# Gated linear attention and a convolution-gated feed-forward: new rules for the planner that orders the instructions, and new priorities

## The chip, the core and the metric

The kernel runs on one core of a Trainium2 chip. A core has five engines with an instruction queue each: TensorE (PE in the profile; its weight loads are PEld), VectorE (DVE), ScalarE (ACT), GpSimd (POOL) and SyncE (SP, which here issues every transfer). Each engine takes its queue strictly in order and waits on semaphores for the others. The metric is the device time of one execution in microseconds (us), the median of several; lower is better.

## The reference, cut to what matters

Inputs: `q`, `k`, `v`, `f_logit` of 4 batches x 8 heads x 768 steps x 48, in float32, and three weights that arrive as 64-bit floats and are split into float32 parts in the kernel.

```python
f = 1.0 / (1.0 + np.exp(-f_logit))
for t in range(768):                       # gated linear attention, state is 48 x 48 per head
    state = f[:, :, t, :, None] * state + np.einsum('bhd,bhe->bhde', k[:, :, t], v[:, :, t])
    y[:, :, t] = np.einsum('bhd,bhde->bhe', q[:, :, t], state)
x = y, heads side by side                  # 4 x 768 x 384
h = np.maximum(x @ w_in, 0.0)              # 384 -> 1024
conv_out = sum over k of conv_w[k] * hp[:, k:k + S, :]   # 3 taps along the sequence, hp is h padded
gate = 1.0 / (1.0 + np.exp(-conv_out))
out = (h * gate) @ w_out                   # 1024 -> 384
```

## The kernel before, in words

**Attention.** The 768 steps of a batch are cut into 6 chunks of 128, which makes 24 chunks in all. For a chunk, SP loads the logits `fb`, the pair k and q as one tile `kq`, and `v`. ACT takes Exp and Ln of the logits (L374, L376; from the tenth chunk on for three chunks at once), DVE forms the running sum along the chunk (the scan, L392), ACT takes the two exponentials `e` (L395, L397), and DVE multiplies them into `kq` (the product, L401). TensorE then multiplies k with q head by head into the one PSUM tile `A` (the score, L418, eight products in sixteen matmul records), and DVE copies the lower triangle of it into `am` (the mask copy, L421). TensorE adds up the output `Y` from the carried state (the carry, L433) and from `am` and `v` (the value step, L440). It also transposes k (L407), which is copied to `kp` by whichever of ACT and DVE is free first (L410), and multiplies it with `v` (the rank step, L462) for the next state, which DVE completes (L469 to L474). ACT and DVE split `Y` into a high and a low part in `xT` (L450, L452). Some rows of `xT` are moved by six small transfers per half batch (L482).

**Feed-forward.** The unit is half a batch, three chunks. Each unit has eight first-layer steps of nine matmuls (L512), one per block of 128 hidden features; each is followed by Relu (ACT, L522), three taps (one on ACT, L528, two on DVE, L532), and for every two blocks a Tanh (ACT, L536) and the gate product (DVE, L538). Each tile of 128 output rows then takes a high part (ACT, L555), a low part (DVE, L559), 24 second-layer matmuls (L568: sixteen with the high part, eight with the low part), a copy (ACT, L574) and a store. There are 64 first-layer steps and 24 tiles.

**Weights.** `w_in` comes in six pieces and `w_out` in eight, as 64-bit floats. `split_f64` turns each piece into a high and a low float32 by a chain of small operations (L287 to L311) that mostly feed each other on DVE; for eleven of the fourteen pieces TensorE joins the low part with three matmuls (L316 to L318, the join).

**What sets the order.** Nothing is issued while the code above runs. Each step becomes an `Op` with an engine (or two to choose from), a duration, a priority key, the steps it needs and the buffers it takes. `Plan.order` then plays the whole program through with a small model: an engine that is free takes the ready step of the lowest key whose buffers are free. `PIPE` is how much before its end a step on ACT or DVE lets the next one start, `LAT` is how long after its end other engines see it. The keys are a step's chunk or unit number plus an offset from the table `CFG` (`f` for the logit loads, `gate` for Exp and Ln, `a` for scan, exponentials and product, `sc` for score and mask copy, `m1` and `m2` for the layers, `w1`, `w1s`, `w2`, `w2s` for weights). The steps are issued in the order in which the plan starts them. In the plan before, a step that needs the result of the step just ahead of it on the same engine may start as early as one that does not (`free[e]`, the time with `PIPE` taken off, is passed as the `"soon"` event).

```python
o.start, o.on, o.end = now, e, now + ns
free[e] = o.end - self.PIPE[e]
seen = o.end + self.LAT[e]
```

Of the kernel before, what the change touches and what calls it, by code (L numbers as in the profile page):

```python
# [11 lines left out]
F32 = mybir.dt.float32  # L12
# [4 lines left out]
AF = mybir.ActivationFunctionType  # L17
ALU = mybir.AluOpType
# [5 lines left out]
F_MIN = 2.0 ** -64  # L24
CFG = dict(lf=3, sg=3, nf=6, groups=[3, 3, 3, 3, 3, 3, 3, 3], f=(-10.52, -14.9), gate=(-0.4, 2.24), kq=-8.44, v=2.32,
           a=5.05, ft=-1.2, b=0.88, sc=-1.11, va=-0.4, st=0.74, ga=-12.99, w1=(-1.96, 2.97),
           w1s=(4.07, 0.42, -5.53, 1.16, 3.36, 1.3), cw=-19.7, w2=(10.23, 8.77),
           w2s=(2.31, 3.44, 5.42, 5.13, 6.56, 6.96, 7.77, 5.53),
           m1=(-1.06, 0.62, 1.0, 0.51, -0.31, 0.54, -0.47, -1.02), m1d=1.83,
           m2=(-0.72, -1.09, 1.03, 0.42, 1.64, -1.82, 0.47, 2.64), m2d=1.96, ez='dddddddddddvvv')  # L30

# [7 lines left out]
class Plan:  # L39

    LOOSE = ("mm", "s", "low", "ob")
    LAT = dict(PE=210, ACT=50, DVE=50, POOL=100, SP=60)
    PIPE = dict(PE=0, ACT=100, DVE=80, POOL=0, SP=0)

# [30 lines left out]
    def order(self):  # L75
        now = 0.0
        free = {e: 0.0 for e in self.LAT}
# [5 lines left out]
        seq = 0  # L83
        done, dma, pipe, mode, table = [], [], 0.0, None, "NE"
        for o in self.ops:
# [4 lines left out]
        while events:  # L90
            now = events[0][0]
            while events and events[0][0] <= now:
                _, _, o = heapq.heappop(events)
# [15 lines left out]
            for e in free:  # L109
# [4 lines left out]
                for o in sorted(ready[e], key=lambda o: o.key):  # L114
# [3 lines left out]
                    for r, i in o.take:  # L118
# [3 lines left out]
                        b = next((b for b in self.rings[r] if not (b[1] & taken)), None)  # L122
# [18 lines left out]
                ns = o.engs[e]  # L141
                if e == "PE":
                    if mode == "r" and o.mode == "f":
                        ns += 95
                    mode = o.mode
                if e == "ACT" and o.mode and o.mode not in table:
                    table = {"N": "N", "T": "TE", "E": "TE"}[o.mode]
# [3 lines left out]
                seen = o.end + self.LAT[e]  # L151
                if e == "SP":
                    pipe = max(o.end + 1500, pipe) + o.size / 0.34
                    seen = pipe + 700
                    dma.append(seen)
                    heapq.heappush(events, (seen, seq, None))
                done.append(o)
                for k, (t, w) in enumerate(((free[e], ("soon", o)), (seen, ("done", o)), (seen, ("free", o)))):
                    seq += 1
                    heapq.heappush(events, (t, seq, w))  # L160
# [11 lines left out]
def gla_moe_kernel(ctx, tc, kq_in, v_in, f_in, w_in, conv_w, w_out, out):  # L172


    nc = tc.nc
# [8 lines left out]
    groups = CFG["groups"]  # L184
# [43 lines left out]
    plan, serial = Plan(), count()  # L228
# [12 lines left out]
    cw = const.tile([P, 3, NF], F32, name="cw")  # L241
# [30 lines left out]
    def split_f64(raw, at, r, n, key, need, hi, lo, nm, mode=None):  # L272
        ids = ("raw", raw), ("ms", nm), ("low", nm), ("mm", "pz" + nm)
        x = n / 512
# [7 lines left out]
        def step(eng, ns, run, need, use=(0, 1), take=()):  # L282
            return plan.op(eng, ns, lambda e: run(e), key, need=need, use=[ids[i] for i in use],
                           take=[(("raw", "ms", "low", "mm")[i], ids[i]) for i in take])

        V, A = nc.vector, nc.scalar
        o = step("ACT", 160 + 500 * x, lambda e: A.activation(ms(0).bitcast(F32), pr(1).bitcast(F32), AF.Abs), [need],  # L287
                 use=(0,), take=(1,))
# [8 lines left out]
                 use=(1,))  # L297
# [6 lines left out]
        if mode == "v":  # L304
            o = step("DVE", 150 + 530 * x, lambda e: V.scalar_tensor_tensor(
                sf(), pr(0).bitcast(U32), 2.0 ** -52, sf(), ALU.mult, ALU.mult), [s])
            o = step("DVE", 150 + 530 * x, lambda e: V.tensor_tensor(mf(), mf(), hi().bitcast(F32), ALU.subtract), [h, o],
                     use=(1,))
            return step("DVE", 150 + 530 * x, lambda e: V.tensor_tensor(lo(), mf(), sf(), ALU.add), [o], use=(1,))
        low = lambda: plan.buf(ids[2])[:, :n]  # L310
# [49 lines left out]
    for g, m in enumerate(groups):  # L360
        fb = ("fb", g)
# [18 lines left out]
    for n in range(N):  # L380
# [13 lines left out]
        ev = lambda z, E=E: buf(E)[:, z].rearrange("p n t -> p (n t)")  # L394
        o1 = plan.op("ACT", 600, lambda e, fv=fv, ev=ev: nc.scalar.activation(ev(0), fv(), AF.Exp), ka, need=[o], use=[fb],  # L395
                     take=[("e", E)], mode="E")
        o2 = plan.op("ACT", 600, lambda e, fv=fv, ev=ev: nc.scalar.activation(ev(1), fv(), AF.Exp, scale=-1.0), ka,  # L397
                     need=[o, o1], use=[fb, E], mode="E")
        keep = plan.op("POOL", 400, lambda e, E=E, b=b, c=c: nc.gpsimd.tensor_copy(ft_all[:, b, c, :], buf(E)[:, 1, :, P - 1]),
# [8 lines left out]

        o = plan.op("PE", 450, turn, kb, need=[ox], use=[X], take=[("s", pt)], mode="f")
        okp = plan.op(dict(ACT=580, DVE=685), 0, lambda e, KP=KP, pt=pt: (  # L410
# [25 lines left out]
        def value(e, c=c, Y=Y, V=V, AM=AM):  # L436
            for p, j in heads:
# [5 lines left out]
        oc = plan.op("PE", 590, carry, kv, need=[stated[n - 1], ox], use=[X], take=[("Y", Y)], mode="f") if c else None  # L443
        ov = plan.op("PE", 1024, value, kv, need=[o, oc, ld_v], use=[V, AM] + ([Y] if c else []),
                     take=[] if c else [("Y", Y)], mode="f")
# [8 lines left out]
        if c < NC - 1:  # L454
# [9 lines left out]

            o = plan.op("PE", 595, rank, ks, need=[ov, okp], use=[KP, V, Y], mode="f")
            ft = ft_all[r, b, c, :].rearrange("p (n o) -> p n o", o=1).broadcast_to([HP + D, NP, D])
# [278 lines left out]
```

## Time and profile before

| what | value |
|---|---|
| time, median of 3 runs | 347.39 us (346.68 to 348.35) |
| the profiled execution's own time | 346.48 us |
| its span, first to last instruction | 344.8 us |
| TensorE busy (records) | 316.0 us, 92% |
| VectorE busy | 282.5 us, 82% |
| ScalarE busy | 237.5 us, 69% |
| GpSimd busy | 24.6 us, 7% |
| mean granted TensorE clock | 0.988 |

The share of busy time is an average over stages. The page's 40 slices show VectorE at nine tenths or more in most slices up to 210 us and at four to eight tenths later, and TensorE the other way round: gaps in the first 50 us, few after 100 us. The transfers move 390 to 410 GB/s in the second to fourth slice (8.6 to 34.5 us) and mostly under 140 GB/s from the sixth on.

### The profile page before, as it was taken

The page shows a single profiled execution, that of the slowest core. Times are in us where ns is not written, and L with a number is a line of the kernel's source. Part 1 is how long each engine was busy: PE and PEld are TensorE (multiplying, and loading weights), DVE is VectorE, ACT ScalarE, POOL GpSimd, SP SyncE. Part 2 cuts the span into 40 slices and gives each one's busy share as a digit, 9 for nine tenths or more (in the row PEclk, how much of TensorE's full clock was granted, in tenths as well). Part 3 has the DMA queues.
Part 4 walks back from the last instruction along what each step waited for, and adds up shares of the span by engine and source line. Part 5 has one row for each costly group of instructions (what it writes and reads, how often), then busy time and mean ns, then how long its engine had stood idle before and what let it go on. Part 6 is the DMA issues. An engine that isn't in the chain of part 4 may idle for free.

```text
span 344.8 us, 6816 instructions
## 1 busy us (share of the span) xinstructions
PE 316.0 (92%) x2703; PEld 285.6 (83%) x2703; DVE 282.5 (82%) x421; ACT 237.5 (69%) x393; POOL 24.6 (7%) x69
## 2 busy tenths in 40 slices
PE   0777879999889999999999999999999999999993
PEld 0654737889779999888989989998998899999993
DVE  7999999999999899998999999249857638879410
ACT  6979767899984694799997785255544637579320
POOL 2110000010100014011001111001000000100000
PEclk9999989999989999999999999999999999999999
DMA  6999732331222303458134304122300021000111
GB/s 225 410 396 393 254 131 84 112 119 67 85 75 67 108 1 108 139 172 274 49 107 120 99 10 131 44 91 94 81 2 2 0 59 47 27 21 1 48 48 53
DMA packets 17452, 37.51 MB, mean 109 GB/s; under 512 B 2540, under 2 KB 8708, under 8 KB 17412
## 3 DMA queue, kind: packets, MB, share of 16 engines
q1 hardware_dynamic: 17412, 37.00, 32.2%
q8 instruction: 23, 0.38, 0.5%
q14 instruction: 17, 0.14, 0.1%
HBM read 29.91 MB, written 4.72 MB: 100 GB/s over the span
## 4 chain that ended last, share of the span: by engine, by line
PE 48%; DVE 39%; ACT 4%; issue 4%; DMA 3%; SPq 1%; DVEq 0%; ACTq 0%
PE mm L568 27%; PE mm L512 13%; DVE g L532 8%; DVE kq L401 5%; DVE am L421 5%; DVE fb L392 4%; DVE g L538 3%; PE Y L440 3%; DVE gx L294 2%; DVE xT L452 2%; DMA fb<-in_f_logit_dram 2%; DVE gx L296 2%; PE A L418 2%; DVE ob L311 1%; PE Y L462 1%
## 5 line engine op out<-in xcount | busy, mean ns | idle before, releaser
L512 PE MATMUL mm<-xT,wi 128*128 128x384 f32 x576 | 108.2, 341 | 2.5 <-ACT hb L522 1.6
L568 PE MATMUL mm<-wo,gx 128*128 128x384 f32 x576 | 107.0, 343 | 0.4 <-ACT hb L522 0.4
L568 PEld LDWEIGHTS mm<-wo,gx 128*128 128x128 f32 x576 | 102.2, 190 | 2.2 <-ACT hb L522 0.7
L512 PEld LDWEIGHTS mm<-xT,wi 128*128 128x128 f32 x576 | 99.1, 188 | 5.6 <-ACT hb L522 2.1
L532 DVE SCALAR_TENSOR_TENSOR g<-hb,cw,g 128x385 f32<-128x385 f32 (+1 forms) x128 | 76.5, 617 | 21.2 <-ACT g L528 18.3
L522 ACT ACTIVATE hb<-mm 128x384 f32<-128x384 f32 x64 | 30.9, 484 | 22.6 <-PE mm L512 22.4
L559 DVE TENSOR_TENSOR gx<-g,gx 128x1024 fp32r<-128x1024 f32 (+2 forms) x28 | 29.8, 1069 | 14.6 <-PE mm L568 13.6
L528 ACT ACTIVATE g<-hb,cw 128x384 f32<-128x384 f32 (+1 forms) x64 | 37.7, 613 | 3.8 <-DVE gx L559 2.1
L555 ACT CAST gx<-g 128x1024 fp32r<-128x1024 f32 (+2 forms) x28 | 25.6, 934 | 20.9 <-PE mm L568 18.8
L418 PE MATMUL A<-kq 48*128 48x128 f32 x384 | 29.4, 295 | 6.5 <-DVE kq L401 4.8
L418 PEld LDWEIGHTS A<-kq 48*128 48x128 f32 x384 | 24.7, 197 | 10.9 <-DVE kq L401 5.5
L536 ACT ACTIVATE g<-g 128x768 f32<-128x768 f32 (+1 forms) x32 | 26.9, 844 | 9.6 <-DVE g L532 9.4
L538 DVE SCALAR_TENSOR_TENSOR g<-g,hb 128x768 f32<-128x768 f32 (+1 forms) x32 | 30.4, 953 | 2.1 <-ACT g L536 2.1
L421 DVE COPY_PREDICATED am<-mask,A 128x1024 f32<-128x1024 uint8 x24 | 31.4, 1308 | 0.3 <-PE A L418 0.3
L392 DVE TENSOR_TENSOR_SCAN fb<-runs,fb 128x512 f32<-128x512 f32 x24 | 28.8, 1216 | 0.9 <-ACT fb L376 0.8
L401 DVE TENSOR_TENSOR kq<-kq,e 128x1024 f32<-128x1024 f32 x24 | 29.0, 1215 | 0.4 <-DMA kq<-in_kq_dram 0.3
L440 PE MATMUL Y<-am,v 128*48 128x128 f32 (+1 forms) x384 | 26.3, 278 | 0.0
L440 PEld LDWEIGHTS Y<-am,v 128*48 128x48 f32 (+1 forms) x384 | 20.5, 129 | 4.3 <-issue 4.2
L574 ACT COPY ob<-mm 128x384 f32<-128x384 f32 x24 | 11.3, 472 | 17.4 <-PE mm L568 16.0
L395 ACT ACTIVATE e<-fb 128x512 f32<-128x512 f32 x24 | 15.0, 625 | 8.2 <-DVE fb L392 5.1
L452 DVE TENSOR_TENSOR xT<-Y,xT 112x512 fp32r<-112x512 f32 x24 | 16.4, 684 | 4.2 <-ACT xT L450 3.3
L450 ACT CAST xT<-Y 112x512 fp32r<-112x512 f32 x24 | 13.9, 580 | 7.7 <-PE Y L440 5.2
(76 smaller groups left out, 285.2 us busy)
## 6 DMA issues: line engine op xcount, KB each, us to landing
kq<-in_kq_dram SPq DMA_DIRECT2D x24, 512.0 KB, 3.6
fb<-in_f_logit_dram SPq DMA_DIRECT2D x24, 256.0 KB, 5.8
v<-in_v_dram SPq DMA_DIRECT2D x24, 192.0 KB, 3.3
out_dram<-ob SPq DMA_DIRECT2D x24, 192.0 KB, 2.0
xT<-in_moe_w_in_dram SPq DMA_DIRECT2D x6, 512.0 KB, 8.7
g<-in_moe_w_out_dram SPq DMA_DIRECT2D x8, 384.0 KB, 6.1
xT<-xT SPq DMA_DIRECT2D x48, 48.0 KB, 2.1
xT<-in_moe_conv_w_dram SPq DMA_DIRECT2D x1, 24.0 KB
```

Source lines behind the costliest of these rows:

```text
L392: o = plan.op("DVE", 1240, lambda e, fv=fv: nc.vector.tensor_tensor_scan(fv(), runs, fv(), 0.0, ALU.mult, ALU.add), ka, need=[gate[n]], us ...
L401: ox = plan.op("DVE", 1222, lambda e, X=X, E=E: nc.vector.tensor_tensor(buf(X), buf(X), buf(E), ALU.mult), ka, need=[o2, ld_x], use=[X, E])
L418: nc.tensor.matmul(buf(("A", n))[:, j, p, :], buf(X)[r, 0, p, :], buf(X)[r, 1, p, :], start=True, stop=True)
L421: o = plan.op("DVE", 1320, lambda e, n=n, AM=AM: nc.vector.copy_predicated(buf(AM), mask, buf(("A", n))), (n, "sc"), need=[o], use=[("A", ...
L440: nc.tensor.matmul(out_of(Y, p, j, w), buf(V).rearrange("p h d -> p (h d)")[:, h * D:h * D + w], buf(AM)[:, j, p, :], start=c == 0 and p < ...
L512: nc.tensor.matmul(buf(ph)[:, :HS], wi[:, t, wl, f * P:(f + 1) * P], x_view(pl, u)[:, t, xl, :], start=(i == 0), stop=(i == 3 * KT - 1))
L522: nc.scalar.activation(hb[:, 2:HS + 2], buf(ph)[:, :HS], AF.Relu, scale=0.5)
L528: o = pl.op("ACT", 620, lambda e, cv=cv, hb=hb, n=n, f=f: nc.scalar.activation(cv(), hb[:, 1:n + 1], AF.Copy, scale=cw[:, 1, f:f + 1]), ke ...
L532: o = pl.op("DVE", 617, lambda e, cv=cv, hb=hb, n=n, f=f, w=w, sh=sh: nc.vector.scalar_tensor_tensor(cv(), hb[:, sh:n + sh], cw[:, w, f:f ...
L538: gates[u, fp] = pl.op("DVE", 960, lambda e, cv=cv, fp=fp, n=n: nc.vector.scalar_tensor_tensor(cv(), cv(), 1.0, h_b[:, fp:fp + 2, 1:n + 1] ...
L559: los.append(pl.op("DVE", 150 + 134 * nn * NF // 128, lambda e, hv=hv, lv=lv, src=src: nc.vector.tensor_tensor(lv(), src(), hv().bitcast(F ...
L568: nc.tensor.matmul(buf(po)[:, :DM], view(g)[:, f, :], wo[:, f, wl, :], start=(i == 0), stop=(i == 3 * NF - 1))
```

## The change

Six things change in the planner and in what it is told; the arithmetic of every step stays as it is.

1. `LAT` and `PIPE` get new values, and a table `OWN` is added: a step that needs the result of another one on the same engine can start only `OWN` after that one's full end (35 ns on DVE, 33 on ACT), where other steps may still start `PIPE` before it.
2. On TensorE the plan charges 95 ns for a change from the mode "r" to "f" and now also 70 ns for the way back, and 1200 ns for a step that starts more than 1500 ns after the last one. The transpose counts as mode "r", no longer "f".
3. The second exponential of a chunk needs only the scan, no longer the first one as well.
4. In the variant "v" of the weight split (three pieces of `w_out`) the subtraction needs only the high part and no longer the scaling in front of it; the last addition needs both.
5. Some durations that the plan is told are new (622 for 600, 410 for 450, 1005 for 1024, 575 for 595 ns).
6. All priorities in `CFG` are new numbers.

```diff
-CFG = dict(lf=3, sg=3, nf=6, groups=[3, 3, 3, 3, 3, 3, 3, 3], f=(-10.52, -14.9), gate=(-0.4, 2.24), kq=-8.44, v=2.32,
-           a=5.05, ft=-1.2, b=0.88, sc=-1.11, va=-0.4, st=0.74, ga=-12.99, w1=(-1.96, 2.97),
+CFG = dict(lf=3, sg=3, nf=6, groups=[3, 3, 3, 3, 3, 3, 3, 3], f=(-8.7, -11.52), gate=(6.01, -13.24), kq=1.28, v=7.74,
+           a=19.28, ft=-1.2, b=-0.52, sc=-0.75, va=0.15, st=-2.21, ga=-17.4, w1=(2.8, 3.89),
...
-    LAT = dict(PE=210, ACT=50, DVE=50, POOL=100, SP=60)
-    PIPE = dict(PE=0, ACT=100, DVE=80, POOL=0, SP=0)
+    LAT = dict(PE=212, ACT=36, DVE=36, POOL=60, SP=60)
+    PIPE = dict(PE=0, ACT=97, DVE=83, POOL=0, SP=0)
+    OWN = dict(PE=0, ACT=33, DVE=35, POOL=40, SP=0)
...
-        done, dma, pipe, mode, table = [], [], 0.0, None, "NE"
+        done, dma, pipe, mode, table, idle = [], [], 0.0, None, "NE", 0.0
...
                 if e == "PE":
-                    if mode == "r" and o.mode == "f":
-                        ns += 95
-                    mode = o.mode
+                    if mode != o.mode:
+                        ns += 95 if o.mode == "f" else 70
+                    if now - idle > 1500:
+                        ns += 1200
+                    mode, idle = o.mode, now + ns
...
-                for k, (t, w) in enumerate(((free[e], ("soon", o)), (seen, ("done", o)), (seen, ("free", o)))):
+                for t, w in ((o.end + self.OWN[e], ("soon", o)), (seen, ("done", o)), (seen, ("free", o)), (free[e], None)):
...
-            o = step("DVE", 150 + 530 * x, lambda e: V.tensor_tensor(mf(), mf(), hi().bitcast(F32), ALU.subtract), [h, o],
-                     use=(1,))
-            return step("DVE", 150 + 530 * x, lambda e: V.tensor_tensor(lo(), mf(), sf(), ALU.add), [o], use=(1,))
+            d = step("DVE", 150 + 530 * x, lambda e: V.tensor_tensor(mf(), mf(), hi().bitcast(F32), ALU.subtract), [h], use=(1,))
+            return step("DVE", 150 + 530 * x, lambda e: V.tensor_tensor(lo(), mf(), sf(), ALU.add), [o, d], use=(1,))
...
-        o1 = plan.op("ACT", 600, lambda e, fv=fv, ev=ev: nc.scalar.activation(ev(0), fv(), AF.Exp), ka, need=[o], use=[fb],
+        o1 = plan.op("ACT", 622, lambda e, fv=fv, ev=ev: nc.scalar.activation(ev(0), fv(), AF.Exp), ka, need=[o], use=[fb],
                      take=[("e", E)], mode="E")
...
-                     need=[o, o1], use=[fb, E], mode="E")
+                     need=[o], use=[fb, E], mode="E")
...
-        o = plan.op("PE", 450, turn, kb, need=[ox], use=[X], take=[("s", pt)], mode="f")
+        o = plan.op("PE", 410, turn, kb, need=[ox], use=[X], take=[("s", pt)], mode="r")
...
-        ov = plan.op("PE", 1024, value, kv, need=[o, oc, ld_v], use=[V, AM] + ([Y] if c else []),
+        ov = plan.op("PE", 1005, value, kv, need=[o, oc, ld_v], use=[V, AM] + ([Y] if c else []),
...
-            o = plan.op("PE", 595, rank, ks, need=[ov, okp], use=[KP, V, Y], mode="f")
+            o = plan.op("PE", 575, rank, ks, need=[ov, okp], use=[KP, V, Y], mode="f")
```

What the new rules and numbers do to the queues is seen in the order in which the instructions stand. In the changed kernel every line number of the weight split is 3 higher (up to the L305 to L309 of before), and those behind it are 2 higher.

The first place is VectorE's queue at the split of the first pieces of `w_in` (the tiles gx_... hold the piece in work, ob_... the low part). Before:

```order
L289 TENSOR_SCALAR gx_244<-gx_244 128x512
L291 TENSOR_SCALAR gx_244<-gx_244 128x512
L289 TENSOR_SCALAR gx_247<-gx_247 128x512
L291 TENSOR_SCALAR gx_247<-gx_247 128x512
L469 TENSOR_TENSOR st_91<-Y,ft_all 112x192
L294 SCALAR_TENSOR_TENSOR gx_244<-xT_154,gx_244 128x512
L296 TENSOR_SCALAR gx_244<-gx_244 128x512
L311 SCALAR_TENSOR_TENSOR ob_283<-xT_154,gx_244 128x512
```

And with the change:

```order
L294 TENSOR_SCALAR gx_206<-gx_206 128x512
L423 COPY_PREDICATED am_87<-mask_84,A 128x1024
L297 SCALAR_TENSOR_TENSOR gx_206<-xT_145,gx_206 128x512
L292 TENSOR_SCALAR gx_236<-gx_236 128x512
L299 TENSOR_SCALAR gx_206<-gx_206 128x512
L294 TENSOR_SCALAR gx_236<-gx_236 128x512
L313 SCALAR_TENSOR_TENSOR ob_255<-xT_145,gx_206 128x512
L297 SCALAR_TENSOR_TENSOR gx_236<-xT_161,gx_236 128x512
```

Before, the steps of one piece stand next to each other, so that a row mostly reads what the row above it wrote; now two pieces, or a piece and the attention, take turns.

The second place is the start of ScalarE's queue (fb_... are the logits, three chunks to a tile; e_... the exponentials). Before:

```order
L374 ACTIVATE fb_105<-fb_105 128x512
L376 ACTIVATE fb_105<-fb_105 128x512
L374 ACTIVATE fb_105<-fb_105 128x512
L376 ACTIVATE fb_105<-fb_105 128x512
L374 ACTIVATE fb_105<-fb_105 128x512
L376 ACTIVATE fb_105<-fb_105 128x512
L395 ACTIVATE e_115<-fb_105 128x512
L397 ACTIVATE e_115<-fb_105 128x512
```

And with the change:

```order
L376 ACTIVATE fb_105<-fb_105 128x512
L378 ACTIVATE fb_105<-fb_105 128x512
L376 ACTIVATE fb_105<-fb_105 128x512 x2
L378 ACTIVATE fb_105<-fb_105 128x512 x2
L376 ACTIVATE fb_106<-fb_106 128x512 x2
L378 ACTIVATE fb_106<-fb_106 128x512 x2
L376 ACTIVATE fb_106<-fb_106 128x512
L397 ACTIVATE e_115<-fb_105 128x512
L378 ACTIVATE fb_106<-fb_106 128x512
L399 ACTIVATE e_115<-fb_105 128x512
```

The first exponential of chunk 1 stood behind six activations on logits and stands behind eleven now, the second behind twelve.

The third place is the start of SyncE's queue, where the loads are issued. Before:

```order
L366 DMA fb_105<-in_f_logit_dram 128x512 x3
L386 DMA kq_107<-in_kq_dram 128x1024
L366 DMA fb_106<-in_f_logit_dram 128x512
L386 DMA kq_108<-in_kq_dram 128x1024
L366 DMA fb_106<-in_f_logit_dram 128x512
```

And with the change:

```order
L368 DMA fb_105<-in_f_logit_dram 128x512 x3
L368 DMA fb_106<-in_f_logit_dram 128x512 x3
L388 DMA kq_107<-in_kq_dram 128x1024
L388 DMA kq_108<-in_kq_dram 128x1024
L329 DMA xT_145<-in_moe_w_in_dram 128x1024 x3
```

All six logit loads of the first two tiles now come ahead of the first `kq`.

More of the change, by code (lines that the diff above doesn't have):

```diff
@@ L24 @@
 F_MIN = 2.0 ** -64
-CFG = dict(lf=3, sg=3, nf=6, groups=[3, 3, 3, 3, 3, 3, 3, 3], f=(-10.52, -14.9), gate=(-0.4, 2.24), kq=-8.44, v=2.32,
-           a=5.05, ft=-1.2, b=0.88, sc=-1.11, va=-0.4, st=0.74, ga=-12.99, w1=(-1.96, 2.97),
[L27 to L30, printed above, removed]
+CFG = dict(lf=3, sg=3, nf=6, groups=[3, 3, 3, 3, 3, 3, 3, 3], f=(-8.7, -11.52), gate=(6.01, -13.24), kq=1.28, v=7.74,
+           a=19.28, ft=-1.2, b=-0.52, sc=-0.75, va=0.15, st=-2.21, ga=-17.4, w1=(2.8, 3.89),
+           w1s=(5.26, -3.21, -10.27, -9.05, -4.36, -8.77), cw=-15.73, w2=(7.75, 23.68),
+           w2s=(2.06, 1.34, 5.56, 4.27, 5.91, 7.08, 13.21, 3.62),
+           m1=(-1.16, -1.36, 1.35, 0.39, 1.88, -0.9, -1.14, -3.36), m1d=2.02,
+           m2=(-1.14, -2.46, -0.57, -4.06, 4.86, 2.1, 2.01, 5.89), m2d=1.05, ez='dddddddddddvvv')
 class Op:
@@ L394, in gla_moe_kernel @@
         ev = lambda z, E=E: buf(E)[:, z].rearrange("p n t -> p (n t)")
-        o1 = plan.op("ACT", 600, lambda e, fv=fv, ev=ev: nc.scalar.activation(ev(0), fv(), AF.Exp), ka, need=[o], use=[fb],
+        o1 = plan.op("ACT", 622, lambda e, fv=fv, ev=ev: nc.scalar.activation(ev(0), fv(), AF.Exp), ka, need=[o], use=[fb],
                      take=[("e", E)], mode="E")
-        o2 = plan.op("ACT", 600, lambda e, fv=fv, ev=ev: nc.scalar.activation(ev(1), fv(), AF.Exp, scale=-1.0), ka,
-                     need=[o, o1], use=[fb, E], mode="E")
+        o2 = plan.op("ACT", 622, lambda e, fv=fv, ev=ev: nc.scalar.activation(ev(1), fv(), AF.Exp, scale=-1.0), ka,
+                     need=[o], use=[fb, E], mode="E")
         keep = plan.op("POOL", 400, lambda e, E=E, b=b, c=c: nc.gpsimd.tensor_copy(ft_all[:, b, c, :], buf(E)[:, 1, :, P - 1]),
```

## The prediction

> **What bounds the kernel now.** I read the page's busy shares and its chain of waits first, then stretches of time, then the rows at the place where the chain changes engines.
>
> ```profile
> PE 316.0 (92%) x2703; PEld 285.6 (83%) x2703; DVE 282.5 (82%) x421; ACT 237.5 (69%) x393; POOL 24.6 (7%) x69
> PE 48%; DVE 39%; ACT 4%; issue 4%; DMA 3%; SPq 1%; DVEq 0%; ACTq 0%
> ```
>
> ```profile
> 0.00:140.54 140.54, 118.73 (x1042) 101.23 (x1044) 134.39 (x219) 110.89 (x194) 13.78 (x41) 0.98 0.47 163
> 140.54:339.14 198.60, 197.22 (x1664) 184.38 (x1663) 148.12 (x203) 126.12 (x199) 10.87 (x28) 1.00 0.23 72
> ```
>
> The columns of the stretches are length, then busy time of PE, PEld, DVE, ACT and POOL with counts, then clock, DMA share and GB/s. Up to 140.54 us VectorE is busy 134.4 of 140.5 us and TensorE 118.7; from there TensorE is busy 197.2 of 198.6. So VectorE sets the pace of the first part, TensorE that of the second. The hand-over is the eleventh mask copy:
>
> ```profile
> 138.78 1.31 DVE L421 COPY_PREDICATED am<-mask,A 128x1024 f32<-128x1024 uint8 x1
> 140.47 1.09 PE L440 MATMUL Y<-am,v 128*48 128x128 f32 x16
> 313.44 25.70 PE L568 MATMUL mm<-wo,gx 128*128 128x384 f32 x144 [0.40 <-ACT hb L522]
> ```
>
> The mask copy ends at 140.09, the value step that reads it follows, and TensorE ends at 339.14; copy, store and end take 5.7 us more, to 344.8. ACT is on 4% of the chain.
>
> This gives a way to price an order without playing it through: the VectorE work that stands ahead of a mask copy or product, plus the TensorE work that stands from its reader to the end, is a **floor** for TensorE's end, and the largest floor counts.
>
> **The price of chained neighbours.** The core of the change is that two instructions of one engine that feed each other no longer stand next to each other where it can be helped. What that is worth shows in VectorE's queue in order of time (start us, duration us):
>
> ```profile
> 20.01 0.40 DVE L289 TENSOR_SCALAR gx<-gx 128x512 f32<-128x512 f32 x1
> 20.44 0.43 DVE L291 TENSOR_SCALAR gx<-gx 128x512 int32<-128x512 int32 x1
> 20.79 0.42 DVE L289 TENSOR_SCALAR gx<-gx 128x512 f32<-128x512 f32 x1
> 21.24 0.43 DVE L291 TENSOR_SCALAR gx<-gx 128x512 int32<-128x512 int32 x1
> 21.58 0.35 DVE L469 TENSOR_TENSOR st<-Y,ft_all 112x192 f32<-112x192 f32 x1
> ```
>
> L291 reads what L289 just wrote: it starts 0.43 us after it, 0.03 after its end. The next L289 works on another piece: it starts 0.35 after the L291, 0.08 before its end. A chained neighbour costs 0.11 us. I went down the order of both kernels and counted the rows whose input is what the row above wrote (for the taps, by the slice): on VectorE 120 before and 30 now, 72 before ahead of mask copy 11, 6 now ahead of mask copy 12. On ACT 50 become 32.
>
> [...]
>
> **VectorE's part of the floor.** I add the mean durations of the groups and take 0.08 off for each instruction behind the first, and put 0.11 on for each chained one. The largest groups:
>
> ```profile
> L532 DVE SCALAR_TENSOR_TENSOR g<-hb,cw,g 128x385 f32<-128x385 f32 (+1 forms) x128 | 76.5, 617 | 21.2 <-ACT g L528 18.3
> L421 DVE COPY_PREDICATED am<-mask,A 128x1024 f32<-128x1024 uint8 x24 | 31.4, 1308 | 0.3 <-PE A L418 0.3
> L401 DVE TENSOR_TENSOR kq<-kq,e 128x1024 f32<-128x1024 f32 x24 | 29.0, 1215 | 0.4 <-DMA kq<-in_kq_dram 0.3
> L392 DVE TENSOR_TENSOR_SCAN fb<-runs,fb 128x512 f32<-128x512 f32 x24 | 28.8, 1216 | 0.9 <-ACT fb L376 0.8
> L410 DVE COPY kp<-ss 128x512 f32<-128x512 f32 x6 | 4.1, 684 | 0.0
> ```
>
> Before, up to mask copy 11: 218 instructions, 145.7 us of durations, less 217 x 0.08 = 17.4, plus 72 x 0.11 = 7.9: **136.3**. The trace has 140.09, so 3.8 us were waits. With the change, up to mask copy 12: 224 instructions, 153.0 us (three scans, three products, a mask copy and a k copy more, four taps and a gate product less, and small ones), less 17.8, plus 0.7: **135.8**.
>
> **TensorE's part.** Starts of neighbours in a stretch without gaps give the prices:
>
> ```profile
> 181.66 0.63 PE L462 MATMUL Y<-v,kp 128*48 128x48 f32 x16
> 182.22 1.16 PE L418 MATMUL A<-kq 48*128 48x128 f32 x16
> 183.31 3.10 PE L568 MATMUL mm<-wo,gx 128*128 128x384 f32 x16
> 186.25 1.75 PE L512 MATMUL mm<-xT,wi 128*128 128x384 f32 x9
> 187.93 0.66 PE L433 MATMUL Y<-kq,st 48*48 48x128 f32 x16
> 188.52 1.09 PE L440 MATMUL Y<-am,v 128*48 128x128 f32 x16
> 189.55 1.83 PE L512 MATMUL mm<-xT,wi 128*128 128x384 f32 x9
> 191.22 1.57 PE L568 MATMUL mm<-wo,gx 128*128 128x384 f32 x8
> ...
> 248.31 0.60 PE L407 MATMUL ss<-ident,kq 128*128 128x128 f32 x4
> 248.66 3.38 PE L512 MATMUL mm<-xT,wi 128*128 128x384 f32 x18
> ```
>
> A rank step takes 0.57, a score 1.09, a carry 0.59, a value step 0.95 (0.9 ahead of a rank step, 1.03 else), a transpose between layer steps 0.35. The last 144 matmuls (25.70 us) make 18 groups of eight at 1.43. A first-layer step is 1.68 from 186.25 to the carry; 1.59 of it is the step and 0.085 the change of mode. Before, from value step 11 on: 57 groups of eight (81.5), 41 layer steps (65.2), 14 value steps (13.3), 13 scores (14.2), 13 transposes (4.6), 11 carries and 11 rank steps (12.9), 41 changes of mode (3.5): **195.2**; the stretch above measured 197.2. Now, from value step 12 on: 54, 43, 13, 12, 10, 10 and 10, and 31 changes, which is 77.2 + 68.4 + 12.4 + 13.1 + 3.5 + 11.7 + 2.6 = **189.0**. Over the whole program the changes of mode fall only from 77 to 73, 0.3 us.
>
> **The floors.** Before 136.3 + 195.2 = 331.5, the largest. Now 324.8 there, 324.8 and 324.7 at mask copies 16 and 17 (164.0 + 160.7, 168.9 + 155.8), and one in the opening is larger: ahead of score 6 stand 71 VectorE instructions, 47.1 - 5.6 + 0.7 = 42.2, and from it 283.4 of TensorE's work, 325.6. So the floor falls by **5.9 us**.
>
> **The opening.** Two more steps move against it: six logit loads go ahead of the first `kq`, and ACT now has eleven activations ahead of the first exponential.
>
> ```profile
> 6.89 0.63 ACT L374 ACTIVATE fb<-fb 128x512 f32<-128x512 f32 x1 [0.29 <-DMA fb<-in_f_logit_dram]
> 8.09 0.61 ACT L395 ACTIVATE e<-fb 128x512 f32<-128x512 f32 x1
> 8.61 0.61 ACT L397 ACTIVATE e<-fb 128x512 f32<-128x512 f32 x1
> 10.61 2.08 PE L418 MATMUL A<-kq 48*128 48x128 f32 x16 [4.77 <-DVE kq L401]
> 13.11 1.31 DVE L421 COPY_PREDICATED am<-mask,A 128x1024 f32<-128x1024 uint8 x1
> ```
>
> The third chunk's Exp stays at 6.89, where its load lands; ten activations at 0.52 (8.09 to 8.61) later the second exponential of chunk 1 starts, at 12.1, and ends at 12.7. The product then starts the score at 14.0 instead of 10.61, and two products and a scan (3.4 us) put the first mask copy at 16.2 instead of 13.11. But VectorE has done 2.3 us more by then (14.0 us of floor work to the end of that copy, not 11.7), so it has lost **0.8 us**, and that delays all floors. Bounds: 0, and 3.1 if none of the work done early counts. The `kq` itself is not late: six loads of 256 KB at 400 GB/s bring it to about 10 us, ahead of 12.7.
>
> **Waits beyond the floor.** TensorE ended 7.6 us after the floor: 3.8 of VectorE's waits, 3.8 behind the hand-over, of which 1.4 are gaps and the rest my prices. One kind is worth a look:
>
> ```profile
> 101.01 1.00 PE L462 MATMUL Y<-v,kp 128*64 128x48 f32 x16 [1.71 <-DVE xT L452]
> 101.94 5.67 PE L568 MATMUL mm<-wo,gx 128*128 128x384 f32 x24
> ...
> 169.24 4.50 PE L568 MATMUL mm<-wo,gx 128*128 128x384 f32 x24
> ```
>
> ```profile
> 101.00:105.00 4.00, 3.99 (x27) 3.90 (x28) 3.85 (x6) 2.89 (x6) 0.00 (x0) 0.57 0.32 59
> ```
>
> After a gap of 1.71 us the clock is 0.57 for 4 us, and a tile takes 5.67 instead of 4.50, 1.2 us more. The plan now prices that and did not before; I take one such spell less, **-1.2**. Bounds: -2.9 (the gap too) and the slow rival below.
>
> **At nothing.** ACT loses two table loads (nine behind the first become seven), 18 chained neighbours, and gains four k copies from VectorE.
>
> ```profile
> L376 ACT ACT_TABLE_LOAD x4 | 5.1, 1283 | 0.1
> L522 ACT ACTIVATE hb<-mm 128x384 f32<-128x384 f32 x64 | 30.9, 484 | 22.6 <-PE mm L512 22.4
> ```
>
> That is 2 x 1.28 + 18 x 0.11 - 4 x 0.59 = 2.2 us less, on an engine that waits 22.6 us for the first layer alone; without that cover it would be worth those 2.2. The k copies' 2.7 us on VectorE are already in the floors, and the three freed subtractions of the weight split are among its unchained rows.
>
> **The sum.** Span 344.8 - 5.9 + 0.8 - 1.2 = 338.5. The execution took 1.7 more than its span, 340.2; the median lies 0.9 above that execution: **341.1**.
>
> **The rivals.**
> *The opening costs its whole delay* (3.1, not 0.8): 343.4. For it: the largest floor now lies there. Against: the scans and products done early stand in every later sum.
> [...]
> *TensorE drops to its slow clock more often,* which ends slower. The new order holds thirteen floors within 1.5 us of the largest (scores 6 and 11, seven joins, mask copies 10, 12, 16 and 17), where the old one held two, so VectorE has no lead at any of them, and a slip there is a gap of 1.7 plus a slow spell of 1.2, 2.9 each. From the third one on the gain is gone: 341.1 + 8.7 = 349.8. For it: a gap of this kind stood before even where the floor was lower. Against: a gap at one floor delays TensorE and so gives VectorE the lead at the next, so that they do not simply add up.
> [...]
> *That the change does not do what it says* is ruled out by the count of 120 and 30.
>
> **Chances and range.** The forecast 0.64; the dear opening 0.14; no effect of neighbours 0.08; the slow clock 0.14, of which 0.03 ends level with one or two gaps. A measurement here tells about 0.5% (1.7 us) from no change: faster than 345.7 is 0.64 + 0.14 = 0.78, level 0.08 + 0.03 = 0.11, slower 0.11. For the range: -1.7 from the other gap, -0.8 from an opening for nothing and about -2 for a price of 0.13 per chained neighbour and fewer waits give 336.5; upward it takes in the dear opening and two slow spells (346.9), 347.5. It leaves out the no-effect rival and the slow one from its third gap on, 0.19.
>
> **What would show it.** Right: mask copy 12 ends near 140 with VectorE's gaps ahead of it under 5 us; the first score near 14; seven table loads behind the first; TensorE ends near 333 with under 2 us of gaps after mask copy 17. Wrong: unchained instructions on VectorE that start 0.03 after their neighbour's end, as chained ones do; gaps over 1.5 us on TensorE beyond 60 us with clocks near 0.6; a first mask copy that starts after 17. The forecast fails if the new order makes VectorE wait more than 6 us longer than the old one did.

## The result, and the profile after

The changed kernel takes **339.19 us** (median, 338.65 to 339.32) against 347.35 for the kernel before on the same chip: a ratio of 0.976, 95% interval 0.9734 to 0.9786, so 8.2 us faster. Taken again in a later series it gave 339.43 us, ratio 0.980 (0.9759 to 0.9841). Forecast were 341.1 us and a gain of 6.3. An execution more than 1.5% above the fastest of its kernel is left out of the medians below; that is one execution each of two experiments.

The profiled execution took 338.65 us with a span of 336.9. From its page, busy times and the chain by engine:

```profile
PE 309.9 (92%) x2703; PEld 284.6 (84%) x2703; DVE 273.2 (81%) x417; ACT 234.0 (69%) x395; POOL 39.3 (12%) x69
PE 58%; ACT 17%; DMA 13%; DVE 8%; issue 2%; SPq 1%; ACTq 0%; DVEq 0%
```

VectorE held 39% of the chain before and holds 8% now; ScalarE's share rose from 4% to 17% and that of transfers from 3% to 13%. Stretches of time, cut at the value step that reads mask copy 12 and at score 6 (length, busy PE, PEld, DVE, ACT, POOL, clock, DMA share, GB/s):

```profile
0.00:141.33 141.33, 121.25 (x1122) 104.54 (x1122) 135.95 (x225) 114.58 (x201) 28.34 (x43) 1.00 0.50 176
141.33:330.87 189.54, 188.68 (x1582) 180.02 (x1581) 137.30 (x193) 118.90 (x194) 10.92 (x26) 1.00 0.21 65
45.64:330.87 285.23, 282.36 (x2406) 264.76 (x2406) 231.08 (x346) 195.65 (x328) 31.23 (x45) 1.00 0.25 79
```

From score 6 at 45.64 to TensorE's end at 330.87 only 2.9 of 285.2 us are without a record of TensorE. So TensorE sets the pace from 46 us on, not from 140: with its work as it is, no faster VectorE or ScalarE could win more than those 2.9 us behind that point. VectorE is nearly full too until mask copy 12, since by the last line less the second it is busy for 93.8 of the 95.7 us from score 6 to the value step. The rows on VectorE and TensorE that correspond to the hand-over and to the first chunk:

```profile
13.36 2.08 PE L420 MATMUL A<-kq 48*128 48x128 f32 x16 [7.52 <-DVE kq L403]
15.49 1.30 DVE L423 COPY_PREDICATED am<-mask,A 128x1024 f32<-128x1024 uint8 x1
...
139.45 1.31 DVE L423 COPY_PREDICATED am<-mask,A 128x1024 f32<-128x1024 uint8 x1
141.33 1.09 PE L442 MATMUL Y<-am,v 128*48 128x128 f32 x16
```

Mask copy 12 ends at 140.76. That is nearly where mask copy 11 ended before: VectorE has one chunk more behind it at the same time, and 189.5 us of TensorE's work are left instead of 198.6. VectorE's rows in the weight split, in order of time:

```profile
20.58 0.67 DVE L297 SCALAR_TENSOR_TENSOR gx<-xT,gx 128x512 int32<-128x512 int32 x1
21.17 0.42 DVE L292 TENSOR_SCALAR gx<-gx 128x512 f32<-128x512 f32 x1
21.50 0.42 DVE L299 TENSOR_SCALAR gx<-gx 128x512 int32<-128x512 int32 x1
21.84 0.42 DVE L294 TENSOR_SCALAR gx<-gx 128x512 int32<-128x512 int32 x1
22.17 0.68 DVE L313 SCALAR_TENSOR_TENSOR ob<-xT,gx 128x512 fp32r<-128x512 uint32 x1
```

Two pieces take turns here, and a row behind one that takes 0.42 us starts 0.33 to 0.34 after it, before its end. Chained, L291 started 0.43 after L289.

### The profile page after: what moved, and what is told of

It reads as the page before. It is cut to its first block, busy times and chain, and to the rows that moved or that the text cites. A ratio compares the mean times of both kernels' runs of the same rounds, so it can differ in the third digit from the quotient of the medians.

```text
span 336.9 us, 6805 instructions
## 1 busy us (share of the span) xinstructions
PE 309.9 (92%) x2703; PEld 284.6 (84%) x2703; DVE 273.2 (81%) x417; ACT 234.0 (69%) x395; POOL 39.3 (12%) x69
## 4 chain that ended last, share of the span: by engine, by line
PE 58%; ACT 17%; DMA 13%; DVE 8%; issue 2%; SPq 1%; ACTq 0%; DVEq 0%
PE mm L570 28%; PE mm L514 19%; DMA g<-in_moe_w_out_dram 5%; PE Y L442 4%; ACT g L530 3%; PE A L420 3%; DMA fb<-in_f_logit_dram 3%; DMA xT<-in_moe_w_in_dram 2%; DMA v<-in_v_dram 2%; PE Y L435 2%; ACT hb L524 2%; ACT g L538 1%; DVE am L423 1%; DVE kq L403 1%; ACT fb L376 1%
## 5 line engine op out<-in xcount | busy, mean ns | idle before, releaser
L570 PE MATMUL mm<-wo,gx 128*128 128x384 f32 x576 | 103.5, 339 | 0.0
L534 DVE SCALAR_TENSOR_TENSOR g<-hb,cw,g 128x385 f32<-128x385 f32 (+1 forms) x128 | 74.4, 614 | 13.1 <-ACT g L530 11.7
L524 ACT ACTIVATE hb<-mm 128x384 f32<-128x384 f32 x64 | 30.6, 487 | 15.6 <-PE mm L514 15.4
L401 POOL COPY ft_all<-e 128x4 f32<-128x4 f32 x24 | 24.1, 1013 | 86.3 <-ACT e L399 86.0
L576 ACT COPY ob<-mm 128x384 f32<-128x384 f32 x24 | 11.4, 475 | 17.8 <-PE mm L570 14.7
L504 POOL COPY hb<-hb 128x4 f32<-128x4 f32 x16 | 12.1, 759 | 88.1 <-DVE g L540 88.0
```

Of the source, the lines that this page charges most:

```text
L524: nc.scalar.activation(hb[:, 2:HS + 2], buf(ph)[:, :HS], AF.Relu, scale=0.5)
L534: o = pl.op("DVE", 617, lambda e, cv=cv, hb=hb, n=n, f=f, w=w, sh=sh: nc.vector.scalar_tensor_tensor(cv(), hb[:, sh:n + sh], cw[:, w, f:f ...
L570: nc.tensor.matmul(buf(po)[:, :DM], view(g)[:, f, :], wo[:, f, wl, :], start=(i == 0), stop=(i == 3 * NF - 1))
```

## The experiments

For each order the floor was worked out as in the prediction. "Excess" is what TensorE's end in the profiled execution lies above it. Each ratio is against the kernel before in the same series, whose median there was 346.5 to 347.4 us; differences in us between two series are uncertain by as much as those medians differ.

| kernel | chained on VectorE | floor | TensorE's end | excess | median us | ratio to before (interval) |
|---|---|---|---|---|---|---|
| before | 120 | 331.5 | 339.1 | 7.6 | 347.35 | |
| VectorE apart, old plan | 60 | 328.1 | 339.0 | 10.9 | 346.71 | 1.002 (0.9986 to 1.0058) |
| the same, further apart | 27 | 326.9 | 342.6 | 15.7 | 351.63 | 1.014 (1.0100 to 1.0184) |
| one low part earlier | 120 | 331.5 | 340.5 | 9.0 | 345.77 | 0.997 (0.9945 to 1.0004) |
| new rules, old numbers | 29 | 332.6 | 340.1 | 7.5 | 347.83 | 1.002 (0.9991 to 1.0056) |
| old rules, new numbers | 122 | 334.1 | 349.7 | 15.6 | 357.38 | 1.030 (1.0253 to 1.0348) |
| **after** | 30 | 325.6 | 330.9 | 5.3 | 339.19 | 0.976 (0.9734 to 0.9786) |
| after, chained again | 117 | 332.0 | 339.1 | 7.1 | 346.54 | 1.000 (0.9969 to 1.0027) |
| after without `OWN` | 121 | 334.8 | 345.9 | 11.1 | 353.84 | 1.022 (1.0164 to 1.0267) |
| after without the idle price | 33 | 334.8 | 341.9 | 7.1 | 351.87 | 1.016 (1.0108 to 1.0203) |
| after, old opening | 30 | 325.6 | 332.8 | 7.2 | 339.90 | 0.980 (0.9749 to 0.9841) |

### Are chained neighbours what it gains by? Chaining the new order again

In the changed kernel, VectorE's queue alone was gone through; where two neighbours were independent and one of the next three rows fed on the first of them, that row was moved up beside it.

```diff
-        for o in self.order():
+        for o in self.neighbours(self.order(), False) if self.tuned else self.order():
```

> The changed kernel with nothing changed but VectorE's queue, in which instructions that feed each other are brought next to each other again (chained neighbours 30 to 117, floor 325.6 to 332.0). Neighbours and floor: 339.2 + 6.4 = 345.6 (344 to 346.5). Neighbours do not matter: 339.2 to 340.

Measured: 346.54 us, level with the kernel before. In its profile:

```profile
0.00:148.30 148.30, 123.60 (x1128) 106.21 (x1130) 140.55 (x225) 115.02 (x202) 17.71 (x43) 0.99 0.49 168
146.45 1.31 DVE L453 COPY_PREDICATED am<-mask,A 128x1024 f32<-128x1024 uint8 x1
```

VectorE does the same 225 instructions ahead of the same point (mask copy 12 and its value step), is busy with them for 140.55 us and not 135.95, and the copy ends at 147.76, 7.0 us later than in the changed kernel. The floor says 6.4, the time 7.4. So 87 more chained pairs cost 0.08 us each in the end, near the 0.11 per pair, since not all of them lie ahead of that copy. The rival that neighbours do not matter is refuted.

### Is it enough to break the chains? Two runs in the old order

The same pass the other way round, on VectorE's queue of the kernel before; the second run looks six rows ahead, not two, and takes rows whose inputs come later.

```diff
-        for o in self.order():
+        for o in self.neighbours(self.order(), True) if self.tuned else self.order():
```

> The kernel before with its own numbers, rules and order on all engines but VectorE; in VectorE's queue an independent instruction is moved between two chained neighbours where one of the next two can be (chained neighbours 120 to 60; floor 331.5 to 328.1). If neighbours cost 0.11 us each and the floor carries it: 347.35 - 3.4 = 343.9 (342.9 to 344.9). If neighbours do not matter and the gain came from the new order as a whole: 347.3, unchanged. If the slow-clock spells were what the change removed: unchanged too, since the gap ahead of the rank step near 100 us stays.

> As the run before it, but looking up to six instructions ahead for one to move: chained neighbours 27, floor 326.9. Neighbours and floor: 347.35 - 4.6 = 342.7 (341.7 to 344), and clearly under the milder version. Neighbours do not matter: 347.3. If moving instructions by hand brings new waits, it comes out above the milder version; that would speak for the plan's timing and not for the neighbours.

Measured: 346.71 us and 351.63 us, no gain and a loss of 1.4%. The first theory missed both. The second run came out above the first, which its expectation takes as a sign for the plan's timing and against the neighbours alone. The profile of the first shows why (a stretch, then three rows of VectorE's queue):

```profile
0.00:140.60 140.60, 117.25 (x1040) 100.07 (x1040) 131.50 (x219) 110.54 (x194) 16.38 (x41) 0.99 0.47 163
```

```profile
37.87 0.36 DVE L502 TENSOR_TENSOR st<-Y,st 112x192 f32<-112x192 f32 x1 [0.62 <-ACT xT L480]
50.83 0.69 DVE L482 TENSOR_TENSOR xT<-Y,xT 112x512 fp32r<-112x512 f32 x1 [0.71 <-ACT xT L480]
53.76 0.56 DVE L324 SCALAR_TENSOR_TENSOR gx<-g,gx 128x384 int32<-128x384 int32 x1 [0.59 <-ACT gx L323]
```

Mask copy 11 ends at 140.2, as before, though VectorE is busy for 131.5 us up to there and not 134.4. What the broken chains saved came back as waits, mostly for ScalarE, whose queue still had the old order: up to there VectorE waited 6.2 us for it, against 1.7 in the kernel before. In the second run the waits grew further (a wait of 1.71 us for a `kq` load, one of 1.55 for an exponential). A floor is a lower bound; here the other queues were not laid out for the lower one. That they would reach it with queues of their own was not tried.

### Rules or numbers? Three partial versions

The new rules and told durations with the old priorities (the edit undoes the table `CFG` alone), the new priorities with the old rules and durations (the new table in the kernel before), and the changed kernel with the `OWN` rule alone taken back. The edits of the first and of the third:

```diff
-CFG = dict(lf=3, sg=3, nf=6, groups=[3, 3, 3, 3, 3, 3, 3, 3], f=(-8.7, -11.52), gate=(6.01, -13.24), kq=1.28, v=7.74,
+CFG = dict(lf=3, sg=3, nf=6, groups=[3, 3, 3, 3, 3, 3, 3, 3], f=(-10.52, -14.9), gate=(-0.4, 2.24), kq=-8.44, v=2.32,
...
```

```diff
-                for t, w in ((o.end + self.OWN[e], ("soon", o)), (seen, ("done", o)), (seen, ("free", o)), (free[e], None)):
+                for t, w in ((free[e], ("soon", o)), (seen, ("done", o)), (seen, ("free", o))):
```

> The new rules and durations with the priorities of before. Chained neighbours 29, but the largest floor is 332.6 (score 13: 120.2 of VectorE + 212.5 of TensorE), 1.1 above the kernel before. Floor: 347.35 + 1.1 = 348.4, at most 1.2 less if waits fall as in the changed kernel (347 to 349). If the count of chained neighbours alone made the gain: about 340.

> The new priorities with the rules and durations of before. Chained neighbours 122, largest floor 334.1. Floor: 347.35 + 2.6 = 350 (348.5 to 351). If the priorities as such made the gain: 339 to 342.

> The changed kernel with all its new numbers and rules, except that a step that needs its neighbour's result on the same engine may again start as early as one that does not. The order has 121 chained pairs on VectorE again and a floor of 334.8 us (the changed kernel: 30 and 325.6). Theory (neighbours cost 0.11 us each and the floor carries it): 334.8 plus the 5.3 to 7.6 us that the two kernels took beyond their floors, plus 6.0 and 1.7 to 2.5 for the tail and what lies around the span: 348 to 351 us. Rival (the gain comes from the other rules and the new priorities): 339 to 341.

Measured: 347.83, 357.38 and 353.84 us. The new rules break the chains with the old priorities too (29 are left), but the order they give has more work ahead of its worst point, a floor of 332.6, and it ends level with the kernel before, as the floor had it. The new priorities without the `OWN` rule are slower than the kernel before, in both versions, and by more than their floors say: either floor allowed 351 us at most. A plan that does not know what neighbours cost expects steps earlier than they come; that the waits stem from this is likely and was not shown apart from the rest of the order. One row of VectorE without `OWN`:

```profile
145.66 0.36 DVE L474 TENSOR_TENSOR st<-Y,st 112x192 f32<-112x192 f32 x1 [3.60 <-PE Y L464]
```

So taking `OWN` back costs 14.7 us with the new priorities (353.84 against 339.19); at TensorE's end it is 15.0, 9.2 of floor and 5.8 of excess. It gives another order altogether, so this is not the price of the chains alone. With the old priorities all the rules together are worth nothing. The gain belongs to neither alone.

### Is the price of an idle TensorE needed?

```diff
-                    if now - idle > 1500:
-                        ns += 1200
```

> The changed kernel without the 1200 ns that the plan charges for a TensorE step after a gap of 1500 ns; the order shifts with it. Chained neighbours 33, but the largest floor is 334.8 (mask copy 11: 112.1 + 222.7). Floor: 339.2 + 9.2 = 348.4 (346 to 350). If chained neighbours alone made the gain: 339.5. If the price on gaps mattered through the clock: gaps over 1.5 us and clocks near 0.6 beyond 60 us.

Measured: 351.87 us, 12.7 slower than with it and above the 350 that its floor allowed. Its order has the floor of 334.8, and it has a gap on TensorE that the changed kernel has nowhere behind 46 us:

```profile
111.54 1.98 PE L440 MATMUL Y<-am,v 128*48 128x128 f32 x16 [5.72 <-DVE am L421]
```

The run does not tell what the rule is worth by itself: without it the priorities give another order altogether, as without `OWN`.

### What does the opening cost?

In the changed kernel, loads, Exp, Ln and the exponentials of the first six and two chunks were put back into the old order in their places of the queues of SyncE, ScalarE and VectorE (here ScalarE's; `g` are the Exp and Ln of a chunk, `e` its exponentials).

```diff
+        new = dict(SP=f[:3] + [kq[0], f[3], kq[1]] + f[4:],
+                   ACT=g[0] + g[1] + g[2] + e[0] + g[3] + e[1] + g[4] + g[5],
...
```

> The changed kernel with the opening's order of before: the first kq ahead of the fourth logit load, the second ahead of the fifth, the first exponentials ahead of the Exp and Ln of chunks 4 to 6, products and scans of VectorE in the old turn; all else stays, floor 325.6. If the opening costs what VectorE loses in waiting, 0.1 us by the trace: 338.7 to 339.5, and the first score near 10.6. If TensorE's late start costs its whole delay (13.36 against 10.61): 336.5.

Measured: 339.90 us, no gain. The first score starts 2.2 us earlier than in the changed kernel, and nothing comes of it:

```profile
11.12 2.08 PE L457 MATMUL A<-kq 48*128 48x128 f32 x16 [5.29 <-DVE kq L440]
16.82 2.08 PE L457 MATMUL A<-kq 48*128 48x128 f32 x16 [1.72 <-DVE am L460]
```

The second score waits for the first mask copy, which starts at 15.49 in either kernel, because the same six scans and two products stand ahead of it on VectorE. The delay of the first score is no cost. The edit does not bring back all of the old opening: in the kernel before only four scans stood ahead of that copy, which started at 13.11.

### One gap less in the old order

In the kernel before, the low part that TensorE waited 1.71 us for at 101 us was moved two places up on VectorE.

```diff
+        n = next(k for k, o in enumerate(q) if o.at == (8, "va"))
+        q.insert(n - 2, q.pop(n))
```

> The kernel before with one VectorE instruction moved two places up: the low part of xT of chunk 9, for which TensorE waited 1.71 us near 100 us and then ran 4 us at clock 0.57. The floor stays at 331.5. If the gap and the slow spell cost what I priced them at, 347.35 - 2 to -2.9 = 344.4 to 345.4. If VectorE's eleventh mask copy sets the pace anyway, 347.0 to 347.4: TensorE gets there earlier and waits for it.

Measured: 345.77 us against 346.97 in that series, ratio 0.997 with an interval that reaches 1.0004: the 1.2 us less are likely, not certain. The gap became 0.81 us and no slow spell follows it in the profiled execution; but that execution lost 2.15 us to a wait in the opening, which the edit does not touch: TensorE's clock became full only at 23.7 us there, at 15.8 in the kernel before.

### Gaps put into the new order

The 17th mask copy, for which TensorE already waited 0.25 us, was moved two and four instructions later on VectorE.

```diff
+        n = [k for k, o in enumerate(q) if o.at[1] == "sc"][16]
+        q.insert(n + 2, q.pop(n))
```

(with `n + 4` in the second)

> The changed kernel with one thing moved: the 17th mask copy goes two instructions later on VectorE, behind a gate product and one tap that it stood ahead of (0.86 and 0.53 us by the starts of their neighbours). TensorE waits 0.25 us for that copy already, so the gap ahead of its value step becomes about 1.65 us, in a part where TensorE alone sets the end. Theory (a gap of this length is followed by a slow spell, as after the 1.71 us gap of the kernel before): granted clock near 0.57 for some 4 us behind it, and 1.4 + 1.2 us longer, 341.8 us. Rival (the clock falls only after a longer gap): clock 1.00 behind it and 1.4 us longer, 340.6. If neither, that is if later leads swallow the gap: 339.2.

> The same copy four instructions later: behind the gate product, two taps and a product (0.86 + 1.06 + 1.13 = 3.05 us), so a gap of about 3.3 us. Theory (slow spell of some 4 us behind it, at the same price whatever the gap's length): 339.2 + 3.05 + 1.2 = 343.4 us. Rival (no slow spell below a longer gap): clock 1.00 and 342.2. If the spell grows with the gap: above 344.

Measured: 343.38 us (341.74 to 345.30) and 345.46 us (343.10 to 346.96), more than either theory gave. The second lies where a spell that grows with the gap was expected (above 344), but the spell in its profile is no longer than others. Rows of TensorE and stretches of the first:

```profile
181.06 1.09 PE L468 MATMUL Y<-am,v 128*48 128x128 f32 x16 [1.78 <-DVE am L449]
```

```profile
38.70:46.10 7.40, 7.40 (x68) 5.40 (x65) 6.73 (x12) 4.10 (x8) 0.00 (x0) 0.54 0.46 129
76.90:80.40 3.50, 3.50 (x13) 3.50 (x12) 3.26 (x7) 2.71 (x6) 0.00 (x0) 0.51 0.02 5
181.00:184.40 3.40, 3.34 (x52) 3.17 (x53) 3.40 (x5) 2.04 (x5) 0.00 (x0) 1.00 0.55 185
```

And of the second:

```profile
178.94 1.97 PE L468 MATMUL Y<-am,v 128*48 128x128 f32 x16 [3.43 <-DVE am L449]
```

```profile
178.80:182.20 3.40, 3.26 (x38) 3.17 (x40) 2.32 (x3) 0.40 (x1) 0.00 (x0) 0.53 0.03 12
```

The gap of 1.78 us is not followed by a slow clock, the one of 3.43 is. But the execution with the gap of 1.78 had two slow spells far ahead of it, where its order is that of the changed kernel and the changed kernel's first profile shows a clock of 1.00. They made mask copy 10 late by 4.2 us at its end, first in this kernel and then in the changed one:

```profile
100.23 1.32 DVE L449 COPY_PREDICATED am<-mask,A 128x1024 f32<-128x1024 uint8 x1
```

```profile
95.94 1.36 DVE L423 COPY_PREDICATED am<-mask,A 128x1024 f32<-128x1024 uint8 x1
```

Behind it only 1.2 us more were lost (TensorE ends at 336.33, 5.5 later). So "a gap of 1.7 costs a spell" is wrong as a rule, and something other than the order decides; the last section shows what. The second one's profiled execution took 343.49, near the first theory's 343.4, but with a spell at 39 us besides the one counted. Why its median lies 2.0 us above that, and the first one's above the forecast, is not settled, since only one execution of each has a trace. More spells would fit: of the second one's executions, the four with mean clocks of 0.976 and 0.977 took 346.27 to 346.96 us, the four with 0.986 to 0.991 took 343.10 to 345.46.

### The changed kernel once more

> The changed kernel once more, nothing edited, in more executions. Its first profiled execution had gaps of 0.67 and 1.30 us on TensorE at 36 to 39 us and no slow spell; the two kernels with a later mask copy have the same order up to there, the same gaps, and a clock of 0.50 from 39 on for 3.4 or 7 us. Theory (whether a short gap is followed by a slow spell differs from execution to execution of one order): mean clocks from about 0.980 to 0.995 among the executions, times from 338.5 to some 342, the median at 339 to 341, and executions with the lower clocks mostly the longer ones. Rival (the spell hangs on the order alone, and the changed kernel is free of it): every execution within 338.6 to 339.4 at a clock of 0.991 or more.

Measured: 338.60 to 341.53 us in six executions, median 339.43, within the theory's bounds; the clocks spread less than it said, from 0.987 to 0.995, and the longest execution is the one with the lowest. The profiled one, of 339.18 us:

```profile
36.02 0.50 PE L320 MATMUL mm<-ob,idr 128*128 128x512 f32 x1 [0.67 <-DVE ob L313]
37.82 0.66 PE L435 MATMUL Y<-kq,st 48*48 48x128 f32 x16 [1.30 <-DVE xT L454]
38.41 1.40 PE L442 MATMUL Y<-am,v 128*48 128x128 f32 x16
...
40.57 2.06 PE L420 MATMUL A<-kq 48*128 48x128 f32 x16
```

```profile
39.00:42.40 3.40, 3.40 (x42) 3.26 (x38) 2.94 (x8) 1.61 (x5) 0.00 (x0) 0.51 0.68 205
```

And the same stretch of the first profile of the changed kernel:

```profile
39.00:42.40 3.40, 3.40 (x51) 2.75 (x47) 3.40 (x8) 2.16 (x5) 0.00 (x0) 1.00 0.59 204
```

The same order, the same gaps of 0.67 and 1.30 us ahead, and once a spell of 3.4 us at half the clock, once none. Whether a short gap is followed by one differs from execution to execution; the rival is refuted. The second profile also has a gap of 1.93 us at 74 us, with no spell behind it. The spell's cost here is small: mask copy 10 ends 1.4 us later, mask copy 12 0.8, and TensorE ends at 331.65, 0.8 later, since part of it falls into VectorE's time.

## Why the prediction was right, and where it was not

The direction, the mechanism and the size hold: forecast 341.1 in a range of 336.5 to 347.5, measured 339.19.

*The price of chained neighbours* (0.11 us) stands. The changed kernel's rows from 21.17 us on, which do not read what their neighbour wrote, start 0.08 to 0.09 before its end, where the chained L291 of before started 0.03 after it; and chaining again cost 7.4 us (346.54 against 339.19).

*The floors* moved as said: 5.9 us. Mask copy 12 ends at 140.76, forecast near 140; from its value step TensorE takes 189.5 us, priced at 189.0. Of VectorE's waits ahead of it there were 5.0 us (140.8 - 135.8), just at the bound of 5 that was given; they were 3.8 before.

*The opening* was mis-sized: I charged 0.8 us. The first score starts at 13.36, not 14.0, and the first mask copy ends at 16.79, with 14.0 us of floor work done by then; that is 2.8 us behind, where the kernel before was 2.7 behind (13.11 + 1.31 - 11.7). So it cost 0.1. Putting back the loads and ScalarE's old order brought nothing. The rival of the dear opening, 3.1 us and 343.4 in all, ends with that and with the measured 339.19.

*The waits beyond the floor* were mis-sized the same way, too high. I took 7.6 us over, less 1.2 for one slow spell. TensorE ended 5.3 above the floor: score 6 starts 3.4 us after its floor (45.64 against 42.2), and 1.9 are lost behind it, where the kernel before lost 3.8 ahead of its hand-over and 3.8 behind. I had attached the 1.2 to a gap and to the plan's new price for it. The runs show that the number of spells differs between executions of one order: the kernel before had two in its profiled execution, the changed one none and then one. That term was right in sign and not for the reason given, so part of the hit is luck.

Together: the opening 0.7 and the waits 1.2 less than forecast, the tail 6.0 and not 5.7: a span of 336.9 for 338.5. The median lies 0.5 above the profiled execution, not 0.9, which is the rest of the 1.9 us.

*The step that was too simple* is the floor as a price for an order. It put VectorE's queue with its chains broken and the old plan at a gain that did not come, and the excess over it runs from 5.3 to 15.7 us in the table. That it worked here because the changed order was planned with `OWN`, so that the other engines were ready when VectorE was, is likely and not shown: the three orders that were planned with `OWN` and not edited by hand have an excess of 5.3 to 7.5 us, the three planned without it 7.6, 11.1 and 15.6. The forecast had taken the excess as a constant, less one spell, and nothing in it had shown that.

*The rivals:* that neighbours do not matter is refuted by the chaining again (339.2 to 340 by that rival, 346.54 measured). That TensorE drops to its slow clock more often did not come: behind 46 us the largest gap is 1.06 us in the first profile and 1.93 in the second, without a spell, where this order ran with thirteen near-equal floors; a late TensorE gives VectorE its lead again, as the 0.8 us left of the spell in the second profile shows. ACT's table loads were seven behind the first, as counted.

## What to carry to other kernels

Where an engine sets the pace, look whether its neighbouring instructions feed each other, and put something independent between them; but plan the other engines' queues for the earlier times as well, or the gain turns into waits. A sum of work ahead of a point and behind it is a lower bound. It priced the chaining of one queue here (6.4 us for 7.4), and not the breaking of its chains, which needs the other queues to follow. The priorities and the rules of the plan were worth something only together: when one is changed, look at the other.

## What the runs showed of the hardware that I had not expected

The slow spells of TensorE in these profiles are near 3.4 us long or a multiple: 3.41 each of the two in the kernel before (from 46.53 and 101.14 us), 3.4 in the second profile of the changed kernel, 6.8 in the one with a gap put in (7.40 us at a mean clock of 0.54 are 6.8 at 0.50), and here with the old rules and new numbers four times as long, around a gap of 9.12 us:

```profile
114.35 7.96 PE L568 MATMUL mm<-wo,gx 128*128 128x384 f32 x29 [9.12 <-DVE wo L309]
```

```profile
106.30:120.00 13.70, 5.65 (x18) 5.66 (x19) 13.60 (x20) 5.00 (x9) 0.76 (x5) 0.51 0.14 31
```

The clock is 0.50 in them; the 4 us at 0.57 that the prediction read in the kernel before are 3.4 us at 0.50. The traces also show where they started. In each of the fourteen profiles every change of the clock lies a whole number of 3.41 us behind the moment at which it first became full: 15.81 us in the kernel before, whose spells start at 46.53 and 101.14, which is 9 and 25 times 3.413 later. In the first profile of the changed kernel it became full at 19.17 and changes only at 333.20, 92 times 3.413 later. Cut along this grid, the two profiles of the changed kernel, the second one first, look like this:

```profile
35.65:39.06 3.41, 1.74 (x29) 1.25 (x31) 3.41 (x8) 3.00 (x6) 0.63 (x1) 1.00 0.86 320
39.06:42.47 3.41, 3.41 (x41) 3.20 (x36) 2.95 (x8) 1.62 (x5) 0.00 (x0) 0.50 0.70 211
```

```profile
36.24:39.65 3.41, 2.02 (x34) 1.53 (x36) 3.41 (x8) 2.72 (x6) 0.62 (x1) 1.00 0.62 225
39.65:43.06 3.41, 3.41 (x48) 2.39 (x48) 3.41 (x10) 2.46 (x4) 0.00 (x0) 1.00 0.61 208
```

The gaps are the same two, but of the first, 0.37 us fall into the stretch in one execution and 0.09 in the other. Of all 1292 stretches at full clock up to TensorE's end, the 14 in which it was busy for less than 1.52 us of 3.41 were all followed by a slow one, of the 19 with 1.52 to 1.92 us 9 were, and of the 1259 with more none. The stretches ahead of the two spells of the kernel before, from 43.11 and 97.73 us, were busy for 1.12 and 1.70 us; of the changed kernel's first profile the least busy stretch is the one above with 2.02. The spell at 39 us in its second profile stands behind a stretch in which TensorE was busy for 1.74 us, with gaps of 0.67 and 1.30. So in these profiles the spells go with how much of one stretch is idle, and a gap near 1.7 us was followed by one or not by where it fell: the 1.71 of the kernel before was, the 1.78 with the mask copy two later was not. What sets the start of the grid, and what decides between 1.52 and 1.92, is not shown.

GpSimd's small copies from `e` into `ft_all` took 443 ns in the kernel before and 1013 in the changed one, in 24 copies each, by the profile, whose times on GpSimd are rough:

```profile
L399 POOL COPY ft_all<-e 128x4 f32<-128x4 f32 x24 | 10.6, 443 | 101.4 <-ACT e L397 101.4
L401 POOL COPY ft_all<-e 128x4 f32<-128x4 f32 x24 | 24.1, 1013 | 86.3 <-ACT e L399 86.0
```

No engine waits for them in the changed kernel. They were slower where VectorE's queue has fewer chains: 425 to 455 ns in the orders with 120 to 122 chained pairs, 576 to 706 in the three whose chains alone were edited, 712 to 1096 in the others planned with `OWN`. What slows them was not tried.
